# Attention weights' transposes moved behind the next query-key products, logits moved last, first places read early

## The chip, the cores and the metric

The kernel runs on one core of a Trainium2 chip. The metric is the device time of one execution in microseconds, the median of three timed runs. One further execution is recorded by the hardware profiler; all rows below come from that one.

## The reference

Three stages follow each other; the change touches the first and the seam to the second.

```python
def _attn_ref(q, k, v):                      # batch 4, heads 8, seq 576, head_dim 64
    scores = scale * np.matmul(q, k.transpose(0, 1, 3, 2))
    mask_plain = (rel >= 0) & (rel < window)                                   # heads 0-3, window 32
    mask_dil = (rel >= 0) & (rel < window * dilation) & (rel % dilation == 0)  # heads 4-7, dilation 4
    scores = np.where(masks[None, :, :, :], scores, -1000000000.0)
    ...                                      # softmax over the last axis
    return np.matmul(attn, v)
...
def _moe_ref(x, expert_emb, tau, w1, w2):    # 2304 tokens, 8 experts, top 1
    logits = xn @ en.T / tau
    expert_idx = np.argmax(logits, axis=1)
    ...
        out[mask] = gate_w[mask, None] * (np.maximum(x[mask] @ w1[e], 0.0) @ w2[e])
...
def _moe2_ref(x, w_in, w_out, alpha):
    h = x @ w_in
    return (np.maximum(h, 0.0) + alpha * np.minimum(h, 0.0)) @ w_out
```

## The kernel before

Attention is cut into 44 units, 11 for each of the 4 batches, numbered `n` from 0 to 43. A unit holds up to four blocks of queries, of the plain heads ("pl", 64 queries and 96 keys for two heads) or of the dilated heads ("dl", 48 queries and 80 keys). Engines run their instructions in the order in which the code is written (the schedule is manual), so the body of the loop over units is the order on TensorE. The stages of a unit:

- `stage_qk(n)`: a mask product and up to four query-key products into the bank `s`; in units 2, 13 and 34 some matmuls on the tile `warm` stand ahead of them (`HEAT`). VectorE takes the maximum (`nm`), ScalarE up to four exponentials (`pe`).
- `stage_t(n-1)`: TensorE transposes the weights `pe` of the unit before into `pt`; one copy takes them to `pts`. For units below 3 it stands behind the query-key products, from unit 3 on ahead of them.
- `stage_av(n-2)`: the products with the values into `o`; VectorE divides into `xs`, SyncE writes `xs` to DRAM (`x_d`).
- `stage_x(n-3)`, the "turns": TensorE transposes `xs` into `psx`, copied to `xp` or `xd`.
- `r_lg`, the logits: eight small products of `xp` and `xd` with the expert embeddings into `psl`, copied to `ls`. In the unit after, `r_lt` transposes `ls` into `psm` and VectorE sums it. There are 12 of each.
- `prep`: transposes of freshly loaded q and k of the batch ahead (`psq`), in lists called `dils` and `plains`; batch 3 has none. `psq`, `psx`, `psl` and `psm` share three banks.

`evac` copies a bank out on whichever of VectorE and ScalarE has the smaller sum of estimated load so far, so another order of the code can give a copy to the other engine.

Routing runs beside attention. When nine of 18 token tiles have their logits, VectorE ranks the tokens (`r_route`) and chooses the first expert (`choose`). `to_table` then issues on GpSimd one scattered write per token tile, in turn into three tables in DRAM (`tab_d`). `regs_a` loads the choice into SyncE's registers, `x_index` reads the first places back from the tables (`ix`), `x_gather` adds the three parts on GpSimd and gathers the rows. `hot(g)` makes, on GpSimd, one-hot compares of four token tiles (`hg` in the table); `hot_rows(g)` multiplies them on TensorE into `lgf` (`hr` in the table). `w_load` and `w_split` (`wl`, `sp`) bring the first expert's weights. The table `last` says after which unit of batch 3, counted from 0 (unit 33), each of these is issued.

After attention the kernel runs nine slots of expert layers (`l1`, `l2`) and four chunks of the dense layers (`m1`, `m2`).

Of the kernel before, what the change touches and what calls it, by code (L numbers as in the profile page):

```python
# [10 lines left out]
I32 = mybir.dt.int32  # L11
# [17 lines left out]
def kernel(  # L29
# [33 lines left out]
    NTAB = 3  # L63
# [5 lines left out]
    const = ctx.enter_context(tc.tile_pool(name="const", bufs=1))  # L69
# [275 lines left out]
    def prep_tiles(b):  # L345
        kpl[b], kdl[b] = ktb[b % 2]
# [291 lines left out]
    n = 0  # L638
# [95 lines left out]
        return tuple(p.tile([128, KD, 512], F32R, tag=nm, name=nm) for nm in ("xh", "xl"))  # L734

    ixs = {}

    def x_index(s_):
        n = -(-WIDTHS[s_] // 128)
        parts = ix_p.tile([128, NTAB, 4], I32, tag="ix", name="ix")  # L740
        for i, tab_d in enumerate(tabs):
            nc.sync.dma_start(out=parts[:, i, 0:n],
                              in_=tab_d[bass.ds(first_row[s_], 128 * n), :].rearrange("(c p) o -> p (c o)", p=128))
        ixs[s_] = parts

    def x_gather(s_):
        if s_ == 1:
            ix = idx
        else:
            if s_ not in ixs:  # L750
                x_index(s_)
            parts, n = ixs.pop(s_), len(chunks_of(s_))

            ix = parts[:, 0]
            for i in range(1, NTAB):
                nc.gpsimd.tensor_tensor(out=ix[:, 0:n], in0=ix[:, 0:n], in1=parts[:, i, 0:n], op=ALU.add)
        for c in chunks_of(s_):
            m = min(128, WIDTHS[s_] - 128 * c)
            t = tmp_p.tile([128, DM], F32, tag="t", name="xg")
            nc.gpsimd.indirect_dma_start(  # L760
                out=t[0:m], out_offset=None, in_=x_d[0:1 + TT * FIRST, :] if s_ == 0 else x_d[:, :],
                in_offset=bass.IndirectOffsetOnAxis(ap=ix[0:m, c:c + 1], axis=0))
            xg[s_, c] = t
# [54 lines left out]
    sp = lambda p: lambda: w_split(0, p)  # L818
    wl = lambda p: lambda: w_load(0, p)
    last = {}  # L820
    hg, hr = (lambda g: lambda: hot(g, nc.gpsimd)), (lambda g: lambda: hot_rows(g))
    for i, f in ((1, open_early), (1, flush), (1, to_table), (2, regs_a), (2, lambda: x_gather(0)), (2, wl(0)), (3, wl(1)),
                 (3, hg(0)), (4, wl(2)), (4, hg(1)), (5, wl(3)), (5, sp(0)), (6, wl(4)), (6, sp(1)), (6, hr(0)), (7, hr(1)),
                 (7, hg(2)), (9, lambda: x_turn(0, 0)), (10, lambda: x_turn(0, 1)), (10, hr(2))):
        last.setdefault(i, []).append(f)
    ends = {3: 0, 6: 1, 10: 2}
    routeq = []
# [13 lines left out]
    for b in range(B):  # L841
        us = units_of(b)
        if b + 1 < B:
            prep_tiles(b + 1)
            prepq += preps(b + 1)
        for i, u in enumerate(us):
            resume()
            for args in free:
                load_qk(*args)
            free.clear()  # L850
            rate[0] = 1 if b < 3 or i > 8 else 2
            if n >= 3:
                route_after(n - 3)
            np_ = PLAN[min(b, 1)][i]
            pq, rq = prepq[:np_], routeq.pop(0) if routeq else []
            prepq = prepq[np_:]
            if i == len(us) - 1 and b < 3:
                while prepq and prepq[0][1] == b + 1 and prepq[0][2] == 0 and prepq[0][4] < 2:
                    pq.append(prepq.pop(0))

            turns = [f for f in rq if f[0] is stage_x]
            lts = [f for f in rq if f[0] is r_lt]
            lgs = [f for f in rq if f[0] is r_lg]
            dils, plains = ([[f for f in pq if (f[4] < 2) == pl and f[2] == h] for h in range(2)] for pl in (False, True))
            assert len(turns) + len(lts) + len(lgs) == len(rq)

            def some(fs, cnt=99):
                for f in fs[:cnt]:
                    f[0](*f[1:])
                del fs[:cnt]  # L870

            late = n < 3
            if n >= 1 and not late:
                stage_t(n - 1)
            stage_qk(n, u)
            some(dils[0], 1)
            some(turns)
            if n >= 1 and late:
                stage_t(n - 1)
            some(lts)  # L880
            some(dils[0])
            some(dils[1])
            some(lgs)
            some(plains[1])
            some(plains[0], 1)
            if n >= 2:
                stage_av(n - 2)
            some(plains[0])
            n += 1
            if b == 0 and i == 3:  # L890
                setup_routing()
            if b == 0 and i == 4:
                setup_emb()
            if b + 1 < B and i == 4:
                load_vpl(b + 1)
            if b + 1 < B and i == 5:
                load_vdl(b + 1)
            to_table()
            if b == 3:
                for f in last.get(i, ()):  # L900
                    f()
# [423 lines left out]
    with tc.If(chunks > 0):  # L1325
        with tc.tile_pool(name="o1", bufs=1) as o1:
# [29 lines left out]
            with tc.For_i(0, chunks, 1) as ci:  # L1356
                ex_ = nc.sync.value_load(rowi[0:1, bass.ds(ci, 1), 0:1], min_val=0, max_val=E - 1)
                rw_ = nc.sync.value_load(rowi[0:1, bass.ds(ci, 1), 1:2], min_val=0, max_val=E * CAP - 128)
                parts = o1.tile([128, NTAB], I32, name="oix")
                ix = parts[:, 0:1]  # L1360
# [94 lines left out]
```

## Time and profile before

| | us |
|---|---|
| three timed runs | 892.4, 893.77, 898.49 (median 893.77) |
| profiled execution, its own time | 902.71 |
| span of that execution's trace | 901.0 |
| outside the span | 1.7 |
| mean granted TensorE clock, of full | 0.951 |

The rows have a start and a duration in microseconds, the engine, the line of the code and the tiles (out<-in); a number in brackets is idle time of the engine ahead of the row and what ended it. "x4" means that four instructions are merged. PEclk is the granted TensorE clock as a share of 2.4 GHz: 1.00 is 2.4 GHz and 0.50 is 1.2 GHz.

### The profile page before, as it was taken

The numbers are of one execution on the slowest core, as the hardware profiler recorded it, in microseconds if no ns is written. First come the engines' busy times: TensorE is split into PE (matmuls) and PEld (weight loads), VectorE is DVE, ScalarE is ACT, GpSimd is POOL, SyncE is SP. The second block draws the span as 40 slices with busy tenths as digits, with TensorE's granted clock in tenths as the row PEclk, the third lists the DMA queues.
The fourth block names the chain that finished last, engine by engine and source line by source line (L and its number), as shares of the span: only waits on it lengthen the run. The fifth ranks groups of instructions, "written<-read, shape, count | busy, mean of one in ns | idle before, by whom it ended". The sixth has DMA issues, their size and how long they took to land.

```text
span 901.0 us, 15220 instructions
## 1 busy us (share of the span) xinstructions
PE 845.7 (94%) x5887; PEld 738.3 (82%) x5887; DVE 464.1 (52%) x965; ACT 378.5 (42%) x817; POOL 202.4 (22%) x211
## 2 busy tenths in 40 slices
PE   6989999889899999999878999999999999999994
PEld 4878877779899999988877888788888888888893
DVE  3566654346465766667568888732332233223330
ACT  3556653334444455536333433533333333333341
POOL 7100012364244465565420000010001000100100
PEclk8899988689999999999998999999999999999997
DMA  9985642427658889879993552110011001000000
GB/s 177 168 173 121 128 78 55 111 79 103 219 106 256 171 168 262 219 173 201 246 205 111 56 192 28 47 48 1 1 57 37 1 1 35 36 1 1 24 24 26
DMA packets 102093, 93.39 MB, mean 104 GB/s; under 512 B 38770, under 2 KB 83076, under 8 KB 102016
## 3 DMA queue, kind: packets, MB, share of 16 engines
q1 hardware_dynamic: 97472, 81.82, 40.8%
q0 software_dynamic: 4544, 10.54, 3.7%
q8 instruction: 48, 0.79, 0.4%
q14 instruction: 29, 0.24, 0.1%
HBM read 77.08 MB, written 15.27 MB: 102 GB/s over the span
## 4 chain that ended last, share of the span: by engine, by line
PE 62%; DVE 14%; DMA 11%; POOL 4%; issue 3%; ACT 3%; SPq 1%; POOLq 0%; ACTq 0%; DVEq 0%
PE mps L1118 18%; PE ops L1144 17%; PE yps L1032 7%; PE hps L809 7%; DMA stg<-in_moe_w_out_dram 3%; DMA stg<-in_moe_w_in_dram 3%; PE s L419 3%; PE pt L437 2%; DMA tab_d<-row,idxi 2%; PE o L458 2%; DMA kld<-in_k_dram 2%; DVE za L1087 2%; DVE zb L1090 2%; PE psq L362 2%; DVE za L1092 1%
## 5 line engine op out<-in xcount | busy, mean ns | idle before, releaser
L1130 DVE SCALAR_TENSOR_TENSOR g<-z,nalpha,g 128x512 f32<-128x512 f32 (+1 forms) x80 | 55.7, 696 | 170.3 <-ACT g L1129 170.3
L1118 PE MATMUL mps<-yh,zhi 128*128 128x512 f32 (+1 forms) x320 | 119.2, 372 | 1.8 <-ACT yh L1108 1.8
L1118 PE MATMUL mps<-yl,zhi 128*128 128x512 f32 (+1 forms) x320 | 119.3, 373 | 1.5 <-DVE yl L1109 1.5
L1118 PE MATMUL mps<-yh,zlo 128*128 128x512 f32 (+1 forms) x320 | 119.0, 372 | 0.0
L1156 POOL DMA_INDIRECT out_dram<-osb,cid x18 | 18.4, 1023 | 410.1 <-ACT osb L1155 378.7
L1128 ACT ACTIVATE z<-mps 128x512 f32<-128x512 f32 (+1 forms) x80 | 44.3, 554 | 150.9 <-PE mps L1118 150.9
L1144 PE MATMUL ops<-zhi,gl 128*128 128x512 f32 x256 | 100.5, 393 | 0.2 <-DVE gl L1132 0.2
L1144 PE MATMUL ops<-zhi,gh 128*128 128x512 f32 x256 | 100.5, 393 | 0.0
L1144 PE MATMUL ops<-zlo,gh 128*128 128x512 f32 x256 | 100.4, 392 | 0.0
L1032 PE MATMUL yps<-hh,whi 128*128 128x256 f32 (+7 forms) x288 | 92.0, 319 | 6.3 <-ACT hh L813 5.3
L727 POOL TENSOR_TENSOR wlo<-stg,whi 128x1024 fp32r<-128x1024 f32 x30 | 76.6, 2553 | 89.6 <-ACT whi L725 77.6
L1032 PE MATMUL yps<-hl,whi 128*128 128x256 f32 (+7 forms) x288 | 89.5, 311 | 4.7 <-DVE hl L814 3.1
L1032 PE MATMUL yps<-hh,wlo 128*128 128x256 f32 (+7 forms) x288 | 89.1, 309 | 0.0
L809 PE MATMUL hps<-xl,whi 128*128 128x256 f32 (+7 forms) x288 | 88.0, 308 | 0.3 <-DVE xl L775 0.3
L809 PE MATMUL hps<-xh,whi 128*128 128x256 f32 (+7 forms) x288 | 88.3, 309 | 0.0
L809 PE MATMUL hps<-xh,wlo 128*128 128x256 f32 (+7 forms) x288 | 87.7, 307 | 0.0
L1118 PEld LDWEIGHTS mps<-yh,zhi 128*128 128x128 f32 x320 | 60.5, 189 | 13.6 <-ACT yh L1108 2.3
L1118 PEld LDWEIGHTS mps<-yl,zhi 128*128 128x128 f32 x320 | 60.6, 189 | 13.5 <-DVE yl L1109 2.0
L725 ACT CAST whi<-stg 128x1024 fp32r<-128x1024 f32 x62 | 64.7, 1043 | 13.6 <-DMA stg<-in_moe_w_dram 13.5
L1118 PEld LDWEIGHTS mps<-yh,zlo 128*128 128x128 f32 x320 | 60.6, 189 | 11.0
L1131 ACT CAST gh<-g 128x512 fp32r<-128x512 f32 x64 | 39.7, 621 | 65.1 <-DVE g L1130 65.1
L1132 DVE TENSOR_TENSOR gl<-g,gh 128x512 fp32r<-128x512 f32 x64 | 44.3, 692 | 44.0 <-ACT gh L1131 43.3
(229 smaller groups left out, 1710.4 us busy)
## 6 DMA issues: line engine op xcount, KB each, us to landing
stg<-in_moe_w_dram SPq DMA_DIRECT2D x64, 512.0 KB
stg<-in_moe_w_in_dram SPq DMA_DIRECT2D x16, 512.0 KB
stg<-in_moe_w_out_dram SPq DMA_DIRECT2D x16, 512.0 KB
yl<-y_d SPq DMA_DIRECT2D x4, 1024.0 KB
kld<-in_k_dram SPq DMA_DIRECT2D x8, 384.0 KB
qld<-in_q_dram SPq DMA_DIRECT2D x8, 384.0 KB
x_d<-xs SPq DMA_DIRECT2D x32, 96.0 KB
vdl<-in_v_dram SPq DMA_DIRECT2D x16, 160.0 KB
```

The costliest lines, as they stand in the source:

```text
L419: nc.tensor.matmul(s[0:nq, i, c0:nk], lhsT=lhsT, rhs=rhs, start=False, stop=(i == m - 1))
L725: nc.scalar.copy(hi, s)
L727: eng.tensor_tensor(out=lo, in0=s, in1=hi.bitcast(F32), op=ALU.subtract)
L809: nc.tensor.matmul(ps, lhsT=parts[j][0][:, kk, :], rhs=parts[j][1][:, kk, 0:wd], start=((kk, j) == steps[0]), stop=((kk, j) == steps[-1]))
L1032: nc.tensor.matmul(ypt[s_, d], lhsT=a[:, 128 * d:128 * (d + 1)], rhs=x, start=(f == 0 and j == 0), stop=(f == NF - 1 and j == 2))
L1118: nc.tensor.matmul(ps, lhsT=a[:, kk, :], rhs=x, start=(kk == 0 and j == 0), stop=(kk == KD - 1 and j == 2))
L1128: nc.scalar.activation(out=z, in_=ps, func=AF.Relu, scale=-1.0)
L1130: vec.scalar_tensor_tensor(out=g, in0=z, scalar=nalpha[:, f:f + 1], in1=g, op0=ALU.mult, op1=ALU.add)
L1131: nc.scalar.copy(gh, g)
L1132: vec.tensor_tensor(out=gl, in0=g, in1=gh.bitcast(F32), op=ALU.subtract)
L1144: nc.tensor.matmul(opt[c, t], lhsT=a[:, 128 * t:128 * (t + 1)], rhs=x, start=(f == 0 and j == 0), stop=(f == NF2 - 1 and j == 2))
L1156: nc.gpsimd.indirect_dma_start(out=out[:, :], out_offset=bass.IndirectOffsetOnAxis(ap=cid[:, 4 * c + t, 0:1], axis=0), in_=o, in_offset=None)
```

## The change

Four edits, all of them of order:

1. `stage_t(n-1)` stands behind `stage_qk(n)` and behind the first dilated `prep` in every unit, the turns behind the remaining `dils`, and `r_lt` right behind the query-key products.
2. `r_lg` stands at the very end of the unit, behind `stage_av` and the last `plains`.
3. `regs_a` and `x_index(0)` are issued after unit 33 (before: unit 35), into a tile of its own (`ix0`), and the gather after unit 34 (before: 35).
4. The compares are issued after units 35, 36 and 37 (before: 36, 37 and 40), their products after units 38, 40 and 41 (before: 39, 40 and 43).

```diff
     ixs = {}
+    ix0 = const.tile([128, NTAB, 4], I32, name="ix0")
...
-        parts = ix_p.tile([128, NTAB, 4], I32, tag="ix", name="ix")
+        parts = ix_p.tile([128, NTAB, 4], I32, tag="ix", name="ix") if s_ else ix0
...
-    for i, f in ((1, open_early), (1, flush), (1, to_table), (2, regs_a), (2, lambda: x_gather(0)), (2, wl(0)), (3, wl(1)),
...
+    for i, f in ((0, regs_a), (0, lambda: x_index(0)), (1, open_early), (1, flush), (1, lambda: x_gather(0)), (1, to_table),
...
-            late = n < 3
-            if n >= 1 and not late:
+            stage_qk(n, u)
+            some(lts)
+            some(dils[0], 1)
+            if n >= 1:
                 stage_t(n - 1)
-            stage_qk(n, u)
-            some(dils[0], 1)
+            some(dils[0])
             some(turns)
-            if n >= 1 and late:
-                stage_t(n - 1)
-            some(lts)
-            some(dils[0])
             some(dils[1])
-            some(lgs)
             some(plains[1])
             some(plains[0], 1)
             if n >= 2:
                 stage_av(n - 2)
             some(plains[0])
+            some(lgs)
             n += 1
```

On TensorE, in batch 3, from the transposes of unit 34 to the values product of unit 33, the order before is:

```order
L437 MATMUL pt<-idf,pe 96x128 x4
L406 LDWEIGHTS e_dl
L406 MATMUL s<-mask_4_188,e_dl 96x320
L419 MATMUL s<-kdl_159,qdl_141 96x48 x4
L513 MATMUL psx<-idf,xs 128x112 x2
L522 MATMUL psl<-xp,enT 32x192
L526 MATMUL psl<-xd,enT 32x2x48 x2
L522 MATMUL psl<-xp,enT 32x192
L526 MATMUL psl<-xd,enT 32x2x48 x2
L458 MATMUL o<-vpl_153,pts 64x65 x8
```

and after the change, on the same engine from the query-key products of unit 35 to those of unit 36 and the transposes of its logits:

```order
L419 MATMUL s<-kdl_159,qdl_141 96x48 x4
L437 MATMUL pt<-idf,pe 96x128 x4
L513 MATMUL psx<-idf,xs 128x112 x2
L458 MATMUL o<-vpl_153,pts 64x65 x8
L522 MATMUL psl<-xp,enT 32x192
L526 MATMUL psl<-xd,enT 32x2x48 x2
L522 MATMUL psl<-xp,enT 32x192
L526 MATMUL psl<-xd,enT 32x2x48 x2
L406 LDWEIGHTS e_dl
L406 MATMUL s<-mask_4_188,e_dl 96x320
L419 MATMUL s<-kdl_159,qdl_141 96x48 x4
L537 MATMUL psm<-idf,ls 128x128
```

The transposes `pt` have gone behind the query-key products `s`, the logits `psl` behind the values product `o`, and between them and the transposes of `ls` only one unit's query-key products are left.

On GpSimd the last two table writes of the second group of token tiles and the places' sums, with the semaphores that they wait for, stood like this before:

```order
L552 DMA tab_d<-row,idxi 18432x1 [waits DMASW4_49]
L552 DMA tab_d<-row,idxi 18432x1 [waits DMASW5_49]
L756 TENSOR_TENSOR ix<-ix 128x2 [waits DMAHW7_49,DMAHW0_49]
L756 TENSOR_TENSOR ix<-ix 128x2 [waits DMAHW1_49,Pool_49]
L760 DMA xg<-x_d,ix 128x512 [waits DMAHW3_49,DMAHW4_49,DMAHW2_49,DMAHW5_49,PE_49,DMAHW6_49,Activation_49,Pool_49]
```

and now, on GpSimd at the same place:

```order
L552 DMA tab_d<-row,idxi 18432x1 [waits DMAHW6_49,DMASW4_49]
L552 DMA tab_d<-row,idxi 18432x1 [waits DMAHW7_49,DMASW5_49]
L757 TENSOR_TENSOR ix_309<-ix_309 128x2
L757 TENSOR_TENSOR ix_309<-ix_309 128x2 [waits Pool_49]
L761 DMA xg<-x_d,ix_309 128x512 [waits DMAHW1_49,DMAHW2_49,DMAHW0_49,DMAHW3_49,PE_49,DMAHW4_49,Activation_49,Pool_49]
```

The semaphores named DMAHW are those of SyncE's transfers: the table writes now wait for the reads of the places, and the sums behind them no longer do.

Further on, on GpSimd behind the gather, the order before is (`rel` and `hot` are the compares, `whi` and `wlo` the first weights' split):

```order
L571 TENSOR_SCALAR rel<-idxf,val_a 128x4
L573 TENSOR_SCALAR hot<-count,rel 128x256 x4
L571 TENSOR_SCALAR rel<-idxf,val_a 128x4
L573 TENSOR_SCALAR hot<-count,rel 128x256 x4
L723 CAST whi<-stg 128x1024
L727 TENSOR_TENSOR wlo<-stg,whi 128x1024
L723 CAST whi<-stg 128x1024
L727 TENSOR_TENSOR wlo<-stg,whi 128x1024
L571 TENSOR_SCALAR rel<-idxf,val_a 128x4
L573 TENSOR_SCALAR hot<-count,rel 128x256 x4
```

and now, on GpSimd behind the gather:

```order
L571 TENSOR_SCALAR rel<-idxf,val_a 128x4
L573 TENSOR_SCALAR hot<-count,rel 128x256 x4
L571 TENSOR_SCALAR rel<-idxf,val_a 128x4
L573 TENSOR_SCALAR hot<-count,rel 128x256 x4
L571 TENSOR_SCALAR rel<-idxf,val_a 128x4
L573 TENSOR_SCALAR hot<-count,rel 128x256 x4
L723 CAST whi<-stg 128x1024
L727 TENSOR_TENSOR wlo<-stg,whi 128x1024
L723 CAST whi<-stg 128x1024
L727 TENSOR_TENSOR wlo<-stg,whi 128x1024
```

The third pair of `rel` and `hot` has moved ahead of the four rows of weights.

## Rows read from the trace of the kernel before

**Rows 1.** The page's busy time, TensorE's line first.
```profile
PE 845.7 (94%) x5887; PEld 738.3 (82%) x5887; DVE 464.1 (52%) x965; ACT 378.5 (42%) x817; POOL 202.4 (22%) x211
```

**Rows 2.** Windows: length, busy PE, PEld, DVE, ACT, POOL (instructions), PEclk, DMA, GB/s.
```profile
28.00:128.00 100.00, 93.39 (x1426) 81.19 (x1425) 63.83 (x214) 62.56 (x180) 0.48 (x1) 0.98 0.70 139
131.00:144.00 13.00, 12.60 (x101) 10.30 (x101) 5.84 (x25) 5.28 (x17) 3.02 (x4) 0.50 0.45 91
162.00:177.00 15.00, 14.43 (x107) 12.56 (x105) 5.69 (x21) 5.29 (x17) 3.06 (x6) 0.50 0.34 84
195.00:206.00 11.00, 10.93 (x90) 9.72 (x91) 3.34 (x17) 3.04 (x7) 2.35 (x4) 0.53 0.26 38
256.00:890.00 634.00, 616.31 (x3267) 542.02 (x3265) 327.54 (x511) 256.20 (x478) 130.07 (x90) 0.99 0.39 95
```

**Rows 3.** TensorE's waits from 28 to 197: total us, times, longest.
```profile
PE lgf L582 <- POOL hot L573: 3.7, 7, 0.7
PE pt L437 <- ACT pe L426: 2.2, 5, 0.9
PE psl L526 <- ACT xd L118: 1.9, 2, 1.3
PE psx L513 <- DVE xs L476: 1.7, 4, 0.5
PE psq L365 <- DVE qdl L115: 1.4, 1, 1.4
PE psq L365 <- DVE kdl L113: 0.9, 3, 0.4
```

**Rows 4.** The tile pt: idle time ahead of its instructions, weight loads included.
```profile
  ACT pe L426: 5.4, 11
```

**Rows 5.** Timeline of TensorE: start, duration, instruction, idle ahead and releaser.
```profile
122.13 0.64 PE L437 MATMUL pt<-idf,pe 128*96 128x128 f32 x4
...
150.06 1.01 PE L437 MATMUL pt<-idf,pe 128*96 128x128 f32 x4 [0.91 <-ACT pe L426]
...
154.32 1.03 PE L419 MATMUL s<-kpl,qpl 128*128 128x96 f32 x8
...
155.60 0.68 PE L458 MATMUL o<-vdl,pts 80*64 80x65 f32 x16
...
160.16 0.28 PE L526 MATMUL psl<-xd,enT 128*32 128x96 f32 x2 [1.30 <-ACT xd L118]
...
166.40 1.86 PE L419 MATMUL s<-kpl,qpl 128*128 128x96 f32 x8
...
168.62 1.13 PE L458 MATMUL o<-vdl,pts 80*64 80x65 f32 x16
...
174.34 0.86 PE L437 MATMUL pt<-idf,pe 96*80 96x96 f32 x4
...
194.18 0.18 PE L582 MATMUL lgf<-idv,hot 128*128 128x2 bf16 x1 [0.72 <-POOL hot L573]
```

**Rows 6.** Timeline of GpSimd, the same columns.
```profile
146.93 0.96 POOL L552 DMA_INDIRECT tab_d<-row,idxi  x1 [0.30 <-issue]
157.54 0.96 POOL L552 DMA_INDIRECT tab_d<-row,idxi  x1 [9.65 <-DVE rs L466]
...
160.06 0.95 POOL L552 DMA_INDIRECT tab_d<-row,idxi  x1 [0.30 <-issue]
172.20 0.19 POOL L756 TENSOR_TENSOR ix<-ix 128x2 int32<-128x2 int32 x1 [11.18 <-DMA ix<-tab_d]
...
176.56 3.63 POOL L573 TENSOR_SCALAR hot<-count,rel 128x256 bf16<-128x256 bf16 x4
```

**Rows 7.** Timeline of SyncE's queue: the three reads of the places.
```profile
168.95 2.09 SPq L742 DMA_DIRECT2D ix<-tab_d  x3
```

**Rows 8.** The chain that ended last, a later table write: start, us.
```profile
204.45 12.04 DMA tab_d<-row,idxi
```

**Rows 9.** Timeline of ScalarE: a copy of the logits.
```profile
143.41 0.33 ACT L118 ACTIVATE ls<-psl 128x192 f32<-128x192 f32 x1 [0.23 <-PE psl L526]
```

More of the change, by code (lines that the diff above doesn't have):

```diff
@@ L821 @@
     hg, hr = (lambda g: lambda: hot(g, nc.gpsimd)), (lambda g: lambda: hot_rows(g))
-    for i, f in ((1, open_early), (1, flush), (1, to_table), (2, regs_a), (2, lambda: x_gather(0)), (2, wl(0)), (3, wl(1)),
-                 (3, hg(0)), (4, wl(2)), (4, hg(1)), (5, wl(3)), (5, sp(0)), (6, wl(4)), (6, sp(1)), (6, hr(0)), (7, hr(1)),
-                 (7, hg(2)), (9, lambda: x_turn(0, 0)), (10, lambda: x_turn(0, 1)), (10, hr(2))):
+    for i, f in ((0, regs_a), (0, lambda: x_index(0)), (1, open_early), (1, flush), (1, lambda: x_gather(0)), (1, to_table),
+                 (2, hg(0)), (2, wl(0)), (3, hg(1)), (3, wl(1)), (4, hg(2)), (4, wl(2)), (5, wl(3)), (5, hr(0)), (5, sp(0)),
+                 (6, wl(4)), (6, sp(1)), (7, hr(1)), (8, hr(2)), (9, lambda: x_turn(0, 0)), (10, lambda: x_turn(0, 1))):
         last.setdefault(i, []).append(f)
```

## The prediction

> **What bounds the kernel now.** I read the busy table first: TensorE is busy 94% of the span [rows 1], so a microsecond taken off its queue counts nearly in full unless something else is late behind it. The windows by stage come next. From 256 us to 890 us TensorE is busy 616.31 of 634.00 us at a clock of 0.99 [rows 2]; the change touches nothing there, so whatever attention saves moves that block forward as it stands. Between 28 and 128 us it is busy 93.39 of 100.00 us at a clock of 0.98 [rows 2]. Attention therefore has two sorts of loss. One is waits: six groups between 28 and 197 us, of 3.7, 2.2, 1.9, 1.7, 1.4 and 0.9 us [rows 3]. The other is the clock: three stretches, 131 to 144, 162 to 177 and 195 to 206 us, stood at 0.50, 0.50 and 0.53, that is at the 1.2 GHz level [rows 2].
>
> What a stretch at 1.2 GHz costs is read off equal work at both levels. Eight query-key instructions took 1.03 us at 154.32 and 1.86 us at 166.40, sixteen value products 0.68 us and 1.13 us [rows 5]: factors of 1.81 and 1.66, so I use 1.7. Of the 14.43 busy us of the second stretch 14.43 x (1 - 1/1.7) = 5.9 us are then loss, of the 10.93 us of the third 4.5 us, of the 12.60 us of the first 5.2 us [rows 2].
>
> **The change part by part.** All sums are made against the profiled execution, 902.71 us (span 901.0 us and 1.7 us around it). It lies 8.9 us above the median of the timed runs, 893.77 us, and I come back to that.
>
> *Transposes behind the query-key products.* The transposes of the weights wait for the exponentials. The list of waits shows 2.2 us in five waits [rows 3], but a wait inside a merged group doesn't show there: the group at 150.06 took 1.01 us, where the same four at 122.13 took 0.64 us [rows 5], so 0.37 us of it is waiting for the second to fourth exponential. Five groups of this sort in the timeline make about 2 us more; the tile's own view, weight loads included, says 5.4 us in eleven waits [rows 4]. I take 4.4 us, between the ends 2.2 and 5.4. With the change, a whole unit's query-key products (some 0.8 to 1.2 us, as at 154.32 with its mask product) run while the exponentials finish. The largest wait, 0.91 + 0.37 = 1.28 us at 150.06, has in front of it unit 34's products and their warm matmuls as well, so I expect all of it to go: **-4.4**. The products that are moved ahead wait for nothing new: their bank is free when the transposes of two units earlier have run, which they still precede. The copy `pts` now queues behind the next exponentials on ScalarE (or moves to VectorE), but its reader is a unit later.
>
> *Logits last.* They wait for the copy `xd`, which stands behind four exponentials on ScalarE: 1.9 us in two waits, 1.30 us of it at 160.16 [rows 3, 5]. Now a values product of 0.68 us [rows 5] and the transposes of 0.64 us lie between. That covers the shorter wait and most of the long one; I leave 0.5 us: **-1.4** (0.6 to 1.9).
>
> *Preps.* The third and fourth user of the three shared banks wait for VectorE's copies, 0.9 us in three waits and 1.4 us in one [rows 3]. The transposes, 0.64 us, now stand between the first and the second dilated prep. The short waits (0.9 us) go, of the long one perhaps 0.3: **-1.2** (0.5 to 1.6). The turns' waits for `xs`, 1.7 us [rows 3], stay: where a unit has no dilated prep, transposes and products still precede the turn, in the other order.
>
> *Transposes of the logits.* Here the change adds a wait. Between `psl` and `psm` only the query-key products are left, about 0.8 to 1.2 us, in which `ls` must be copied. That copy takes 0.33 us on ScalarE and started 0.23 us after its product [rows 9], so it should fit; but TensorE is in order, and whenever it is late, the transposes of the weights, the turns and the values product queue behind `psm`. No row shows the new order. From below it costs nothing, from above the longest wait behind ScalarE, 1.30 us [rows 5], in each of 12 units: 15.6 us. The nearest row is the copy that started at once, so I take **+0.7** for all twelve.
>
> *One-hot products.* TensorE waits 3.7 us for GpSimd's compares [rows 3], one tile of four at a time, 0.72 us each [rows 5], because compares (3.63 us for four, [rows 6]) and products stand too close. GpSimd gets to the first compares at 176.56 only because the places are read at 168.95 [rows 6, 7]. With the places read early, GpSimd can go from the last table write, ending at 161.0, straight to the sums and the gather (172.20 to 176.1 in the rows, 3.9 us) and the first compares (4.1 us with `rel`): done at 169.0. The read itself has to wait for the ninth table write, issued at 146.93. The reads of the next three waited in the same way: writes issued from 157.54, read at 168.95, so a write takes up to 11.4 us to land [rows 6, 7], and a later one took 12.04 us [rows 8]. That puts the first read at 155 to 156 and its data some 3 us later (168.95 to 172.20), at 158 to 159, and the table writes at 157.54 now queue behind it on GpSimd, as do the gather and compares: 0.5 to 1.5 us late. So compares at 169.5 to 170.5, by a chain of DMA times that does not get shorter when TensorE does.
>
> The first product now stands after unit 38, whose transposes started at 174.34 [rows 5]. The waits above that vanish between the first table write and unit 38 are some 4.3 us, so TensorE arrives at about 170: no wait, if the stretch from 162 stays at 1.2 GHz. The other two products have two and one units (4 to 6 us and 2 to 3 us) per set of 4 us, and arrive with less than 0.5 us to wait. **-3.7**, and 0 to -3.7 as the range.
>
> The Trainium skill, page "DMA: Bandwidth & Descriptors", section "Anatomy of one DMA — SWDGE (gpsimd) path", gives a DMA issued from GpSimd a fixed time of about 2.0 us. By that the places could be read at 149 us, GpSimd would never be late, and the term would be -3.7 at either clock. The rows say five times as much [rows 6 to 8], and I go by the rows.
>
> Sum of the waits: -4.4 - 1.4 - 1.2 + 0.7 - 3.7 = **-10.0 us** (from -4 to -13; the far end of the logits' wait is a rival below).
>
> *The clock.* The third stretch at 1.2 GHz began right behind the waits for the compares of 0.72 us at 194.18 [rows 2, 5]. With those gone I expect it to go too, 4.5 us. But the timed runs are 4 to 10 us shorter than the profiled one with no other difference than the profile, so they may lack a stretch already; I count half, **-2.3 us**. The second stretch began behind the waits at 156 to 160 us, the 1.30 us one the longest [rows 5], and would also be worth 5.9 us, but not here: at 2.4 GHz TensorE would be at the first one-hot product near 165 us and stand there until 169.5 to 170.5 for GpSimd. That gives back 4.5 to 5.5 us. I count nothing for it.
>
> **Forecast.** -12.3 us on 902.71 us is 1.4%. Taken off the median that is 881.5 us; I say 882.
>
> **The rivals.**
>
> *Waits alone (25%).* The waits go, the clock falls as often as before, or the timed runs never had the third stretch: 893.8 - 10.0 = 883.8 us. For it: the first stretch, 131 to 144, has causes that the change leaves alone.
>
> *More clock (15%).* The stretch from 162 goes too and the table writes land sooner than 11 us, so that GpSimd is not late: up to 5.9 us more and the whole third stretch, 893.8 - 10.0 - 4.5 - 5 = 874 us. Against it are the 11.4 us above.
>
> *The compares' wait moves forward (18%).* TensorE comes to unit 38 early, waits 4 to 5 us for the first compares, and the clock falls behind that wait as it did behind the ones at 194. Then the 3.7 us are not won, another stretch of 1.2 GHz costs about 4.5 us where the old third one did, and 5.9 us of the second one are won: 893.8 - 6.3 + 4.5 - 4.5 + 1.3 is about 889 us. This is the change not doing what its one-hot part says.
>
> *Slower: the logits' copy is late in every unit (6%).* ScalarE takes the next unit's exponentials or a `pts` copy first, and each of 12 units waits for `ls` right behind its query-key products. The price is 12 waits; at (10.0 + 0.7) / 12 = 0.9 us each the gain of the waits is used up, at the 1.30 us of [rows 5] with the clock of an added stretch (5 us) it is 893.8 - 10.7 + 15.6 + 5 = 904 us. Against it: 0.33 us for the copy, started after 0.23 us [rows 9].
>
> **How the numbers follow.** The forecast has 36%, the rivals 25, 15, 18 and 6%. One per cent, 8.9 us, is about what a measurement of this kernel can tell from no change, since its three timed runs alone span 6.1 us. Faster by over 1% means below 884.8 us: most of the forecast (29 of 36), half of the waits alone (12), all of "more clock" (14), little of the compares' rival (2): 0.57. Slower by over 1% is above 902.7: the slow rival, half of it, and a little for a clock that falls oftener: 0.06. The rest, 0.37, is within 1%. The range leaves out the best of "more clock" and the slow rival: 872 to 895 us.
>
> **What would show it.** In the new profile the waits of `pt` for `pe` should be gone from the list, those of `lgf` under 0.5 us in sum, those of `psl` under 1 us; `psm` should wait under 0.3 us a time for `ls`. The places should be read near 155 us, the first compares end near 169, and the windows show at most two stretches at 0.5 between 128 and 210 us. The end of attention (the first expert product, `hps`) should come about 10 to 15 us before where it was. The prediction is wrong if `psm` waits in most of its 12 units, if `lgf` waits several microseconds after unit 38, or if the granted clock falls in places where it stood at 1.00 before.

## The result, and the profile after

| | before | changed |
|---|---|---|
| median of 13 runs each | 895.12 us | 885.32 us |
| lowest and highest | 889.43, 901.87 | 879.64, 895.71 |
| ratio of the times, 95% interval | | 0.988 (0.9852 to 0.9908) |
| profiled execution, its own time and span | 902.71, 901.0 | 888.99, 887.2 |
| first expert product `hps` in it | 197.17 us | 187.38 us |

The forecast was 1.4% and 882 us; measured is 1.2%, which on its base of 893.77 us is 883.0 us. The sum came out nearly right, but two of its terms were too small and one had the wrong sign. In all ratios of this document executions of more than 1.5% above the fastest of the same kernel are left out, so a ratio need not be the quotient of the medians beside it.

The waits of TensorE in the profile of the changed kernel from 28 to 190 us, with total us, times and the longest, answer to [rows 3]:

```profile
PE lgf L582 <- POOL hot L573: 9.4, 4, 7.3
PE psx L513 <- ACT qdl L118: 1.7, 1, 1.7
PE psx L513 <- DVE xs L476: 1.0, 2, 0.6
PE o L458 <- ACT pts L118: 1.0, 1, 1.0
PE psx L513 <- DVE key_a L325: 0.9, 1, 0.9
PE psl L526 <- ACT xd L118: 0.4, 1, 0.4
PE psq L365 <- DVE qpl L115: 0.2, 1, 0.2
```

The waits of `pt` for `pe` are gone, `psl` has 0.4 us left of its 1.9 for `xd`, and `psm` does not wait. VectorE's copy `qdl`, for which `psq` waited 1.4 us, is now one of ScalarE's, and the turn behind it waits 1.7 us. The wait for the compares has not gone: it grew from 3.7 to 9.4 us, 7.3 us of it in front of the very first product.

The list of waits shows only part of what the new order saved. In the groups of instructions, the busy time of a group contains the waits of its second and later instructions. These are TensorE's groups from 28 us to the first `hps`, first of the kernel before (to 197.17), with busy us and mean ns, then idle us ahead of them:

```profile
L437 PE MATMUL pt<-idf,pe 96*80 96x96 f32 (+1 forms) x164 | 28.9, 294 | 2.3 <-ACT pe L426 2.2
L522 PE MATMUL psl<-xp,enT 128*32 128x192 f32 x44 | 9.5, 367 | 0.0
L526 PE MATMUL psl<-xd,enT 128*32 128x96 f32 x88 | 6.2, 266 | 2.4 <-ACT xd L118 1.9 <-ACT pe L426 0.4
```

and of the changed kernel (to 187.38):

```profile
L437 PE MATMUL pt<-idf,pe 96*80 96x96 f32 (+1 forms) x164 | 24.4, 272 | 0.0
L522 PE MATMUL psl<-xp,enT 128*32 128x192 f32 x44 | 7.2, 355 | 0.0
L526 PE MATMUL psl<-xd,enT 128*32 128x96 f32 x88 | 6.1, 262 | 0.5 <-ACT xd L118 0.4
```

The counts are equal. The transposes of the weights lost 4.5 us of busy time besides their 2.3 us of idle time, the logits 2.4 us besides 1.9. So 6.8 us came from the first edit's transposes and 4.3 us from the logits' new place, where the prediction had 4.4 and 1.4.

The mean granted clock of the whole stretch is 0.89 in both profiles, but not the same work fell into the stretches at 1.2 GHz: 29 of the 164 transposes before, 18 after. So the work at full clock is looked at by itself. From 71 to 128 us the clock stood at 1.00 in both kernels; the transposes of the weights in this window, first before, then changed (length, busy time and count, granted clock, share of the DMA engines, GB/s):

```profile
71.00:128.00 57.00, 9.52 (x62) 1.00 0.59 118
71.00:128.00 57.00, 9.09 (x66) 1.00 0.59 120
```

That is 154 and 138 ns each. Over all transposes up to `hps` that started at full clock it is 164 and 138 ns. Worked out with these, about 3.5 of the 4.5 us are waits that went and about 1 us is the clock; of the logits' 2.4 us about 0.5 us is the clock.

How far the wait in front of the first one-hot product goes back is seen in the timelines. GpSimd's in the changed kernel (start, us, instruction, idle ahead and its releaser), to be held against [rows 6, 7]:

```profile
128.19 1.08 POOL L552 DMA_INDIRECT tab_d<-row,idxi  x1 [100.74 <-DVE rs L466]
...
149.29 0.96 POOL L552 DMA_INDIRECT tab_d<-row,idxi  x1 [0.30 <-issue]
158.11 0.96 POOL L552 DMA_INDIRECT tab_d<-row,idxi  x1 [7.86 <-DVE xs L476]
...
165.72 3.63 POOL L573 TENSOR_SCALAR hot<-count,rel 128x256 bf16<-128x256 bf16 x4
```

The queue of SyncE in the same kernel:

```profile
150.59 7.04 SPq L743 DMA_DIRECT2D ix<-tab_d  x3
```

and TensorE's timeline in the same kernel:

```profile
166.71 0.19 PE L582 MATMUL lgf<-idv,hot 128*128 128x2 bf16 x1 [7.31 <-POOL hot L573]
...
187.38 0.67 PE L810 MATMUL hps<-xh,whi 128*128 128x192 f32 x4
```

GpSimd came out at the predicted times: table writes held back to 158.11 (predicted 158 to 159 for the data of the read), first compares done at 165.72 + 3.63 = 169.35 (predicted 169.5 to 170.5). The steps on the way were others: the first read was issued at 150.59, not at 155 to 156, and the three reads took until 157.63 to be issued, where 3 us had been counted for their data; the two errors cancel. The row at 158.11 names VectorE's `xs` as the releaser. That write also waits for the reads, and in the second profile of this kernel, below, its row names the read. TensorE did not come when predicted: it was there at 166.71 - 7.31 = 159.40, not at 170. The windows show why, beside [rows 2] (length, busy TensorE, weight loads, VectorE, ScalarE, GpSimd, granted clock, share of the DMA engines, GB/s):

```profile
48.00:71.00 23.00, 23.00 (x234) 20.56 (x234) 11.44 (x44) 8.72 (x29) 0.00 (x0) 0.55 0.73 147
71.00:128.00 57.00, 55.95 (x898) 49.08 (x893) 38.16 (x123) 37.97 (x114) 0.00 (x0) 1.00 0.59 120
128.00:161.00 33.00, 30.14 (x393) 24.60 (x393) 20.44 (x84) 17.11 (x63) 10.90 (x12) 1.00 0.32 54
161.00:175.00 14.00, 6.16 (x58) 5.23 (x59) 1.64 (x5) 1.67 (x6) 12.46 (x18) 0.52 0.94 114
188.00:195.00 7.00, 7.00 (x56) 6.10 (x56) 2.59 (x12) 1.86 (x6) 2.06 (x2) 0.51 0.17 39
243.00:877.00 634.00, 617.31 (x3260) 542.16 (x3258) 324.49 (x511) 255.70 (x477) 128.92 (x91) 0.98 0.39 95
```

The stretch at 1.2 GHz from 131 to 144 us, which the prediction kept, is gone: 128 to 161 us ran at 1.00. TensorE ran up to the first product at full speed, waited, and stood at 0.52 until 175 us. But 48 to 71 us, which in the kernel before had 0.93, now stands at 0.55. The last block is as busy as before, 617.31 of 634.00 us for 616.31 [rows 2]. `hps` came 9.8 us earlier, and the medians are 9.8 us apart; that the two agree is chance. The two profiled spans are 13.8 us apart, because what lies behind `hps` was also 4.0 us shorter (703.8 and 699.8 us), where the change touches nothing; in another execution of the changed kernel, below, it was 693.1 us.

### The profile page after: what moved, and what is told of

Read it like the earlier page. It is cut to its first block, busy times and chain, and to the rows that moved or that the text cites. A ratio compares the mean times of both kernels' runs of the same rounds, so it can differ in the third digit from the quotient of the medians.

```text
span 887.2 us, 15233 instructions
## 1 busy us (share of the span) xinstructions
PE 836.1 (94%) x5887; PEld 731.7 (82%) x5887; DVE 459.3 (52%) x959; ACT 375.7 (42%) x823; POOL 200.1 (23%) x211
## 4 chain that ended last, share of the span: by engine, by line
PE 70%; DMA 10%; DVE 9%; ACT 5%; issue 3%; POOL 2%; SPq 1%; POOLq 0%; ACTq 0%; DVEq 0%
PE mps L1116 21%; PE ops L1142 21%; PE hps L810 8%; PE yps L1030 7%; DMA stg<-in_moe_w_out_dram 3%; DMA stg<-in_moe_w_in_dram 3%; PE s L419 2%; PE o L458 2%; DMA kld<-in_k_dram 2%; DMA stg<-in_moe_w_dram 2%; ACT pe L426 1%; PE pt L437 1%; PE s L405 1%; PE psq L362 1%; PE psx L513 1%
## 5 line engine op out<-in xcount | busy, mean ns | idle before, releaser
L426 ACT ACTIVATE pe<-s,nm 96x80 f32<-96x80 f32 (+1 forms) x168 | 42.0, 328 | 77.2 <-DVE nm L421 56.8
```

Of the source, the lines that this page charges most:

```text
L426: nc.scalar.activation(out=pe[0:nq, i, :], in_=s[0:nq, i, :], func=AF.Exp, bias=nm[0:nq, i:i + 1])
```

## The experiments

The theory: the order of the unit saves waits one by one, and the first one-hot product ends up waiting for a chain on GpSimd that starts with the first table write. The rivals: the clock made the gain, or the early places alone did. Ratios are to the kernel before, run on the same chip beside each group of kernels; its medians were 890.98 us beside order only, places only and the two with later products, 892.84 beside changed again, logits as before and the two with a fill, and 897.73 beside the other three. Medians of different groups are not to be compared.

| kernel | median us (runs) | ratio, 95% interval | `hps` at | waits of `lgf`, us |
|---|---|---|---|---|
| changed, again | 880.3 (6) | 0.9862 (0.9801 to 0.9924) | 178.95 | 4.5 |
| order only | 888.48 (12) | 0.9981 (0.9945 to 1.0017) | 190.34 | 7.2 |
| places only | 889.39 (12) | 0.9935 (0.989 to 0.9981) | 188.76 | 3.1 |
| products late | 879.67 (6) | 0.9877 (0.9834 to 0.992) | 180.75 | none |
| products behind | 882.78 (12) | 0.9899 (0.9861 to 0.9937) | 185.14 | none |
| logits as before | 892.45 (12) | 1.0006 (0.9974 to 1.0038) | 197.43 | 4.3 |
| logits early | 889.48 (10) | 0.9952 (0.9906 to 0.9998) | 194.03 | 2.7 |
| logits' transposes late | 886.97 (4) | 0.9887 (0.9841 to 0.9933) | 191.83 | 3.2 |
| transposes alone | 885.86 (4) | 0.9845 (0.9782 to 0.9909) | 190.25 | none |
| fill in unit 6 | 879.07 (7) | 0.984 (0.9796 to 0.9884) | 187.97 | 8.5 |
| late and fill | 877.13 (6) | 0.9808 (0.9759 to 0.9857) | 185.00 | none |

For changed again and for places only the profile puts the waits of `lgf` down to `issue`, which names nothing, and for the three kernels with other places of the logits most of them. The first product started 0.99 to 1.00 us after its compares in each of these, as in the profiles that name GpSimd, so they are counted as waits for the compares.

### The changed kernel once more

> The changed kernel itself once more, beside the others of this set. Expected by every theory: 0.985 to 0.991 of the kernel before. Its second profile shows which stretches at 1.2 GHz come again: by the theory that they follow waits, the one from 48 us on (behind the wait of 1.72 us in unit 6) and the one behind the wait for the first compares come again, at the same two places; by the rival, that they come anywhere, others do.

The ratio repeats, 0.9862. Of the two stretches at 1.2 GHz that the expectation asks for, the one behind the wait for the compares came again, shorter (160 to 166 us); the long one from 48 us on did not, though the wait of 1.7 us for `qdl` did. Four of some 3 us each came instead, from 44, 54, 122 and 149 us on. The profile shows a different execution: first `hps` at 178.95, 8.4 us ahead of the first profile of the same program. GpSimd's timeline in it:

```profile
120.06 1.07 POOL L552 DMA_INDIRECT tab_d<-row,idxi  x1 [91.95 <-DVE rs L466]
...
147.89 0.96 POOL L552 DMA_INDIRECT tab_d<-row,idxi  x1 [7.82 <-DMA ix<-tab_d]
...
156.82 3.63 POOL L573 TENSOR_SCALAR hot<-count,rel 128x256 bf16<-128x256 bf16 x4
```

and TensorE's:

```profile
157.81 0.18 PE L582 MATMUL lgf<-idv,hot 128*128 128x2 bf16 x1 [2.39 <-issue]
...
178.95 0.67 PE L810 MATMUL hps<-xh,whi 128*128 128x192 f32 x4
```

From the first table write to the end of the first compares it takes 160.45 - 120.06 = 40.4 us here and 169.35 - 128.19 = 41.2 us in the other profile. The chain has a length of its own, 38.6 to 44.4 us in the eleven profiles with the new places; its start moves with TensorE. What TensorE waits is that length less its own time from the same point to the first product: 159.40 - 128.19 = 31.2 us there, at full clock, and 155.42 - 120.06 = 35.4 us here, with stretches at 0.57 from 122 to 126 and 149 to 153 us. In the kernel before, the first write started at the row below and the compares were done at 176.56 + 3.63 = 180.19 [rows 6], 52.7 us later, so the chain lost 11.5 to 12.3 us. Edits 3 and 4 alone take it to 39.6 us (places only, below), the order alone to 46.0 us, because VectorE then has the rows of the tenth write ready 23.7 us behind the first write (149.92) and not 30.0 us (157.54, [rows 6]). The row is GpSimd's timeline of the kernel before:

```profile
127.52 1.07 POOL L552 DMA_INDIRECT tab_d<-row,idxi  x1 [101.81 <-DVE rs L466]
```

### The order alone, the places alone

The first kernel has the new unit body with the old table, the second the new table with the old body.

The second, against the changed kernel:

```diff
+            late = n < 3
+            if n >= 1 and not late:
+                stage_t(n - 1)
             stage_qk(n, u)
-            some(lts)
             some(dils[0], 1)
-            if n >= 1:
+            some(turns)
+            if n >= 1 and late:
                 stage_t(n - 1)
+            some(lts)
             some(dils[0])
-            some(turns)
             some(dils[1])
+            some(lgs)
...
             some(plains[0])
-            some(lgs)
```

> The kernel before with the new order of the unit's stages (edits 1 and 2) and the old table (places read after unit 35, compares and products where they were). Theory: with the stages' waits gone TensorE outruns the chain of table writes, reads of the places, gather and compares, which is made of DMA times and does not shorten. TensorE would be at the first one-hot product (after unit 39) near 163 us, the first compares end near 180 us: a wait of about 15 us or more, the waits of pt, psl and psq gone, and a time of 893 to 902 us (no gain, or slower). Rival, that each part's waits simply add: the 7 to 8 us of pt, psl and psq are won whatever the table says, 885 to 888 us.

> The changed kernel with the old order of the stages (edits 3 and 4 alone). Theory: TensorE keeps the waits of pt, psl and psq (about 7 us), comes to unit 38 later and so waits less than 3 us for the first compares; the 3.7 us of before go in part: 889 to 893 us. Rival, that the early places carry the gain: 884 to 887 us, as the changed kernel.

The order alone gives nothing that can be told from no change (0.9981), close to what was expected, but not by a wait of 15 us. Its `hps` came at 190.34, 6.8 us earlier than before, in spite of 7.2 us of waits for the compares; these were early, at 168.62, because the table writes had come at 149.9 to 154.9. The clock in this profile was 0.86 on average up to `hps`, with 1.2 GHz from 169 to 186 us behind that wait. That the clock took the rest is likely but not shown: the profile that the 6.8 us are counted from, of the kernel before, was itself 7.6 us longer than the median of its kernel. The places alone give 0.65%, but by the medians of all executions, 889.39 and 890.98, only 0.2%. The two come to 0.8% by themselves (0.5% by all medians) and to 1.2 and 1.4% together; the intervals do not show more than a sum.

### The products further behind

In the first kernel the first product goes behind unit 42, the two others behind attention, and the weights' split ahead of the second and third compares. In the second only the products move, all behind units 42 and 43.

The first table, against the changed kernel (the products `hr(1)` and `hr(2)` follow in later steps, behind attention):

```diff
-                 (2, hg(0)), (2, wl(0)), (3, hg(1)), (3, wl(1)), (4, hg(2)), (4, wl(2)), (5, wl(3)), (5, hr(0)), (5, sp(0)),
-                 (6, wl(4)), (6, sp(1)), (7, hr(1)), (8, hr(2)), (9, lambda: x_turn(0, 0)), (10, lambda: x_turn(0, 1))):
+                 (2, hg(0)), (2, wl(0)), (3, wl(1)), (4, wl(2)), (4, sp(0)), (5, wl(3)), (5, sp(1)), (6, hg(1)), (6, wl(4)),
+                 (7, hg(2)), (9, hr(0)), (9, lambda: x_turn(0, 0)), (10, lambda: x_turn(0, 1))):
```

The second, in place of the same two lines:

```diff
+                 (2, hg(0)), (2, wl(0)), (3, hg(1)), (3, wl(1)), (4, hg(2)), (4, wl(2)), (5, wl(3)), (5, sp(0)),
+                 (6, wl(4)), (6, sp(1)), (9, hr(0)), (9, lambda: x_turn(0, 0)), (10, lambda: x_turn(0, 1)),
+                 (10, hr(1)), (10, hr(2))):
```

> The changed kernel with the one-hot products taken further behind (the first after unit 42, the second and third among the first expert's layers) and, on GpSimd, the two weight splits ahead of the second and third compares. Theory: the 9.4 us of waiting for the compares and the stretch at 1.2 GHz behind it go, lgf waits under 2 us: 874 to 879 us. Rival, that the end of attention is bound by what follows on GpSimd (weights, places of the second slot): the wait only moves, to whi or to the gather behind, 883 to 887 us.

> The changed kernel with the one-hot products alone further behind (after units 42 and 43), GpSimd's own order as it is. Theory: the compares' wait of 9.4 us shrinks to under 5 us, but the weights' split stands behind all three compares (it ended at 183 us) and the first expert product waits for it, so only a part comes: 879 to 884 us. Rival, that TensorE waits for GpSimd in the same sum wherever the products stand: 885 us, within 2 us of the changed kernel.

The wait for the compares is gone in both, and the idle time up to `hps` fell from 15.16 us in the first profile of the changed kernel to 8.71 and 9.01. TensorE still waits, for what comes next. In the first kernel, then in the second:

```profile
PE psl L526 <- issue: 3.0, 1, 3.0
```

```profile
PE psm L537 <- ACT ls L118: 2.9, 1, 2.9
PE psl L522 <- issue: 1.4, 1, 1.4
```

The times, 0.9877 and 0.9899, are not below those of the changed kernel. The expected 874 to 879 us of the first was just missed, the 879 to 884 us of the second held. So the 9.4 us that the profile shows there are not 9.4 us that a better place gives back: its other profile has 4.5, and 3 to 4 us turn up at the next in line.

### The logits' two halves

The first kernel puts logits and their transposes back to where they stood among the turns and preps. The second and third put back one of them; the fourth moves nothing but the weights' transposes, so that the dilated preps stand between the turns and the logits again. All have the new table.

The first, against the changed kernel:

```diff
             stage_qk(n, u)
-            some(lts)
             some(dils[0], 1)
...
             some(turns)
+            some(lts)
             some(dils[1])
+            some(lgs)
...
-            some(lgs)
```

The fourth, against the changed kernel too:

```diff
             stage_qk(n, u)
-            some(lts)
             some(dils[0], 1)
...
                 stage_t(n - 1)
-            some(dils[0])
             some(turns)
+            some(lts)
+            some(dils[0])
             some(dils[1])
+            some(lgs)
...
-            some(lgs)
```

> The changed kernel with the logits and their transposes where they were (edit 2 and the move of the logits' transposes undone). Theory: the waits of psl for xd come back, 1 to 2 us, but TensorE then waits that much less for the first compares, whose end does not depend on it: within 2 us of the changed kernel. Rival, that the waits add: 1.5 to 2.5 us slower than the changed kernel.

> The changed kernel with the logits alone back behind the turns and the dilated preps, and the logits' transposes where the change has them. Theory (the first edit took the dilated preps out from between the turns and the logits, so that the logits wait for the copies xd, 5.6 us in the kernel with both back): waits of psl 4 to 6 us and about 892 us (887 to 896), a ratio of 0.995 to 1.005. Rival (the loss of that kernel was its stretch at 1.2 GHz, 46 to 74 us, which comes and goes): psl waits as much but the time is 880 to 887 us wherever the stretch is short.

> The changed kernel with the logits' transposes alone back behind the turns, and the logits last in the unit. Theory: psl waits under 1 us, psm not at all, and the time is that of the changed kernel, 879 to 887 us. Rival (the place of the logits' transposes was what counted): about 890 us with waits of psx or psm of over 2 us.

> The new places in the table, and of the order only the weights' transposes moved behind the query-key products and the first dilated prep; turns, logits' transposes, preps and logits stand to each other as in the kernel before. Theory: psl waits about 2 us as before, since a prep stands between turns and logits again, and the time lies between the changed kernel and the one with early logits, 884 to 889 us. Rival (clock): as the two others, with no order among the three.

The expectation of the first failed, and its rival too: with logits as before the whole gain is lost, 1.0006. Its waits up to 190 us show a part of where:

```profile
PE psl L526 <- ACT xd L118: 3.1, 3, 1.3
PE psx L513 <- ACT qdl L118: 1.7, 1, 1.7
PE psl L522 <- ACT kdl L118: 1.5, 1, 1.5
PE psm L537 <- ACT kdl L118: 0.9, 1, 0.9
PE psl L522 <- DVE xd L113: 0.6, 1, 0.6
```

The products into `psl` wait 5.6 us in all (two waits of 0.2 us are not among these lines), against 2.3 before. The first edit puts the dilated preps ahead of the turns; before, part of them lay between the turns and the logits and gave the copies `xp` and `xd` their time. With the logits back behind the turns that cover is missing. This is not the whole loss of 12 us: the logits cost 5.2 us of idle and 2.1 us of busy time more than in the first profile of the changed kernel, and the compares 5.1 us less. The rival is the clock: over its twelve executions it was 0.9573, over the six of the changed kernel beside it 0.9635, which at 7.0 us for 0.01 (worked out below) is some 4 us. The rest is open. With the logits alone back, 0.9952, about half of the loss is there, but not as expected: `psl` waits 2.4 us, not 4 to 6, and the turns `psx` 6.6 us instead of 3.9; its clock stood at 1.2 GHz from 43 to 74 us too, so it does not tell the waits from the clock. With their transposes alone back, 0.9887, nothing is lost, though `psl` waits 1.8 us and `psm` 0.8 us, more than expected. Between these two the intervals still touch (0.9906 to 0.9998, 0.9841 to 0.9933); only the kernel with both back is clear of the changed one.

The group of the first logits' products tells the two places apart whatever the clock did. In the kernel with both back:

```profile
L522 PE MATMUL psl<-xp,enT 128*32 128x192 f32 x44 | 9.3, 355 | 2.4 <-ACT kdl L118 1.5 <-DVE xd L113 0.6 <-ACT xp L118 0.2
```

Its busy time is 9.2 to 9.5 us in the five kernels with early logits (before, places only, both back, logits early, transposes alone) and 7.1 to 7.6 us in those with the logits last that were read (changed twice, order only, products late, transposes of the logits late, late and fill), at mean clocks from 0.85 to 0.93. In the same way `pt` has 28.1 and 28.9 us where it stands ahead of the query-key products and 23.6 to 25.6 us behind them. Over the transposes that started at full clock this is 164 and 168 ns each ahead of them and 137 to 139 ns in the eleven profiles behind them, so here the place is the cause.

"Transposes alone" was expected to lie between and, in four executions, does as well as the changed kernel, 0.9845. It waits for the logits,

```profile
PE psl L526 <- ACT xd L118: 2.2, 2, 1.3
PE psl L522 <- ACT kdl L118: 1.6, 2, 1.4
PE psl L522 <- ACT pe L426: 0.6, 1, 0.6
```

4.4 us, but not at all for the compares: arriving later, it finds them done. So, as far as this goes, edit 2 makes good for what edit 1 had displaced, and an order that displaces nothing does without it. That the waits of the logits and of the compares take each other's place here is read from one profile of each kernel. These waits do not put the kernels in the order of their times: `psl` waits 4.4 us here and 2.4 us in the slower kernel with early logits.

### A fill for the wait in unit 6

The wait of 1.72 us for `qdl` stands in unit 6 at 45 us, just ahead of the stretch at 1.2 GHz. The first kernel puts eight products of the tile `warm` in front of that unit's turns; they compute nothing that is used. The second has the late products as well.

```diff
+            for _ in range(8 if n == 6 else 0):
+                nc.tensor.matmul(lgf, lhsT=warm[:, 0:128], rhs=warm, start=True, stop=True)
             some(turns)
```

> The changed kernel with eight matmuls on the warm tile, 512 columns each, put into the wait of unit 6 ahead of its turn (they write a bank that nothing has used yet; about 1.7 us at 2.4 GHz, as long as the wait). Theory, that the stretch at 1.2 GHz from 48 us on follows this wait: the stretch goes or shrinks to a few us; units 7 to 12 run some 9 us sooner, of which the wait for the first compares takes a part back, since their chain does not move as much: 878 to 883 us, 3 to 7 us under the changed kernel. Rival, that the stretch has another cause: it stays and the time is within 2 us of the changed kernel or up to 2 us longer.

> The products far behind and the weights ahead, as in the third experiment, and the eight warm matmuls in unit 6. Theory: with no products to wait for, the whole 9 us of the stretch come through: 870 to 875 us. Rival, that the stretch has another cause: 879 to 881 us as without the warm matmuls.

The wait is gone and the stretch is not; it begins some 4 us later. Windows of the first kernel's profile, which comes from the longest of its seven executions (887.59 us), and one of the second's (883.48 us):

```profile
28.00:52.00 24.00, 22.99 (x370) 19.50 (x367) 16.48 (x61) 15.89 (x47) 0.45 (x3) 1.00 0.97 201
52.00:76.00 24.00, 24.00 (x207) 21.61 (x208) 10.28 (x31) 10.01 (x31) 0.00 (x0) 0.50 0.47 93
```

```profile
50.00:71.00 21.00, 21.00 (x182) 18.92 (x183) 9.08 (x29) 8.64 (x26) 0.00 (x0) 0.51 0.64 126
```

So the stretch comes without that wait, and in the second profile of the changed kernel the wait came without the long stretch: it is neither needed nor enough. The time of the first kernel, 879.07 us, lies in the range expected with the stretch gone, for another reason or in executions that were not profiled; the second lies above its 870 to 875 us. "Late and fill" has the best ratio of all, 0.9808, but its interval touches that of the changed kernel (0.9852 to 0.9908) and overlaps that of its repetition; a gain over the changed kernel is not shown.

## Why the prediction held, and where it did not

The number held and the account behind it only in part. Of the three signs by which the prediction was to be wrong, two came: `lgf` waited 7.3 us behind unit 38, and the clock fell where it had stood at 1.00, from 52 to 69 us. That the number came out is in good part luck: two terms mis-sized by 5.3 us together made up for part of the 9.4 us by which the one-hot term was off (from -3.7 to +5.7).

- **Transposes behind the query-key products, -4.4.** Mechanism right, size too small: -6.8 us, about 1 us of it the clock. The profile's tile view counted 5.4 us in eleven waits [rows 4], but a wait inside a merged group sits in the busy column, and I took five such groups of some forty.
- **Logits last, -1.4.** Mechanism right, mis-sized: -4.3 us, 2.4 of them inside the groups, about 0.5 us of these the clock. I had also not seen that edit 1 takes the preps away from between turns and logits, so that without edit 2 these waits are not 2.3 but 5.6 us.
- **Preps, -1.2.** `psq` lost 2.6 of its 2.8 us of idle time, the turns gained 0.8 and `o` 1.0: -0.8 us. The long wait stayed, for a copy that `evac` had moved to ScalarE.
- **Transposes of the logits, +0.7.** 0.0 and 1.3 us in the two profiles. The slower rival, `ls` late in each unit, did not happen.
- **One-hot products, -3.7.** This is the step that failed: +5.7 us in the first profile (9.4 for 3.7), +0.8 in the second. "TensorE arrives at about 170" was worked out from the 1.2 GHz stretches of the one profile; without the one at 131 to 144 us it came at 159.40. This is the mechanism of the third rival, the compares' wait moved forward, to which I gave 18% and 889 us. Its 889 us were too high because the order saved more than I had summed, and by the sum itself: -6.3, a new stretch in place of the old (+4.5 - 4.5), +4.5 for the wait and -5.9 for the second stretch give 886 us; its last term, +1.3, is about the difference of the last two with the wrong sign. "By a chain of DMA times that does not get shorter when TensorE does" was half right: 40 to 41 us long in these two profiles, but it starts when TensorE and VectorE let it. The 11.4 us for a table write to land were too long too: the first read was issued 4.6 us after the write that it waits for.
- **Clock, -2.3.** The mean granted clock is 0.958 over the 58 runs of the kernel before and 0.960 over 19 of the changed one; within each kernel, 0.01 goes with 7.0 us (a straight line fitted through all runs). That makes 1.0 us. Side by side on one chip it is 0.9635 over the six runs of the repetition and 0.9588 over the 16 of the kernel before, some 3 of the 12.5 us between them. So most of the gain is not the clock's; by these two counts its part is 1 to 3 us. In the first profile the stretches moved; from 28 to 206 us the mean clock was 0.88 as before.

Measured terms of the first profile: -6.8 - 4.3 - 0.8 + 0.0 + 5.7 = -6.2 us of the 9.8. The other 3.6 us lie in groups that got shorter, for the most part because the stretches at 1.2 GHz fell on other work: of the 128 plain query-key products (19.8 to 17.9 us) 28 started at 1.2 GHz before and 11 after, at about the same time for one at full clock, 131 and 134 ns. No experiment holds the stretches fixed. How much of the 9.4 us the timed runs pay is open too, since the two kernels without that wait are not faster.

## What to carry to other kernels

When waits are collected for a sum, take idle and busy time of a group together: 6.9 of the 11.1 us that the transposes and the logits saved stood in the busy column, all but some 1.5 us of it as waits of the later instructions of a group. A step that is moved takes its cover away from its neighbours, so ask what it stood between. And a product that depends on a long chain on another engine should be placed by the length of that chain from the point where both start, at the full clock, not by the arrival time of one profile; here that removed the wait, and a shorter time was not shown.

## What the runs showed of the hardware

The granted clock stayed low for long stretches of continuous work. In the changed kernel TensorE was busy 23.00 of 23.00 us from 48 to 71 us at 0.55; with the logits as before it was this, 44 to 75 us:

```profile
44.00:75.00 31.00, 30.89 (x283) 27.83 (x284) 13.67 (x48) 12.32 (x37) 0.00 (x0) 0.51 0.55 118
```

The kernel before, with the old order and more idle time there, had a clock of 0.93 from 48 to 71 us:

```profile
48.00:71.00 23.00, 21.83 (x333) 19.19 (x329) 14.81 (x53) 13.22 (x38) 0.00 (x0) 0.93 0.79 155
```

The Trainium skill, page "TensorE: Matmul & The Clock Gate", section "Part 1: The HAM clock gate (the "warmup" mystery)", says that the clock is set by how busy TensorE has been of late. By itself this does not explain these rows: TensorE is busy throughout by its records, and the clock stays at the 1.2 GHz level. What keeps the clock down there, whether the kind of work, which is short transposes and products in 32-bit numbers, or something else, was not tested. The same program had this stretch in one profile and two short ones of 3 us each (44 to 47 and 54 to 57 us) in the other.

Reads and writes of the small tables are slow one after the other. In the changed kernel the three reads of 1 KB were issued from 150.59 on, 4.6 us after the first table's last write at 145.98, and the next write could be issued 7.5 us later, at 158.11. The Trainium skill's page "DMA: Bandwidth & Descriptors", section "Anatomy of one DMA — SWDGE (gpsimd) path", which the prediction weighed, gives a write from GpSimd a fixed time of about 2.0 us. The 4.6 us between such a write and the read that waits for it are more than twice that.
